# First batch of an attention and expert kernel: W1 fetched in row chunks, its projection split by head group, and the first layer run without other matmuls in between

## The chip, the cores and the metric

The kernel runs on one core of one Trainium2 chip, as one launch. The metric is the device time of that launch in microseconds (us). TensorE does the matmuls (PE in the profile, its weight loads PEld), VectorE is DVE, ScalarE is ACT, GpSimd is POOL, and SyncE (SP) issues most transfers.

## The reference

A linear attention over 32 memory slots feeds a mixture of experts in which every token goes to one expert:

```python
a = softmax(phi, axis=seq)                                # B, H, S, 32
k_m, v_m = einsum(a, k), einsum(a, v)                     # B, H, 32, 64
attn = softmax(q @ k_m.T / sqrt(64))                      # B, H, S, 32
x = (attn @ v_m) transposed to (B * S, H * 64)            # tokens
logits = normalized(x) @ normalized(expert_emb).T / tau
e = argmax(logits); gate = softmax(logits)[e]
out[token] = gate * (relu(x @ w1[e]) @ w2[e])             # w1: 512 x 1024, w2: 1024 x 512
```

There are B = 8 batches of S = 576 tokens, H = 8 heads and 8 experts.

## The kernel before, in words

The program goes through the batches one after the other. For each batch it computes the slot sums, the scores, the attention weights `aw` (softmaxed and transposed by DVE), and picks one expert for the whole batch. Since a token is its attention weights times `v_m`, `x @ w1` is computed as `aw @ (v_m @ w1)`: the **projection** (tiles `pg`, copied by ACT into `gh` and by DVE, as the rounding rest, into `gl`) multiplies the 32 slots of each head by W1, and the **first layer** (tiles `ph`) multiplies the attention weights `aT` by `gh` and `gl`. The second layer (tiles `py`) uses W2 in a rounded part `wh` and a rest `wl`, both made on POOL and ACT (`split_w`).

The eight heads form two groups g of four. In the projection each head is a matmul with 64 rows and 32 columns of the array, and `heads` gives each of the eight heads a place (row half, column quarter) of its own; the four heads of one group take four of these eight places. W1 of the chosen expert is four chunks c of 128 rows by 1024 columns in `w1s`; group 0 reads chunks 0 and 1, group 1 reads chunks 2 and 3. The projection has two column halves k of 512; a tile `pg_kg` is one half of one group.

The first layer makes 16 tiles, `ph_sf` (token half s, eighth f of the 1024 features), six matmuls each; after each one ACT writes `hh` (for s = 1 also `h4`) and DVE writes the rest `hl`. It is a generator: `batch` calls the steps that are listed for number n after tile n, and this hand-written list sets the order of all other work on every engine. The tiles `pg`, `tt` and `ph` share four PSUM banks in turn (`mm`), so a tile waits until the one four turns earlier has been read.

Only batch 0 is touched. There, `pairs` multiplies `aw` by `vv` for five token tiles i and two groups g (tiles `po`, 40 matmuls), from which DVE makes the logits `lg` and the best expert `oh`; `turned` transposes `aw` (tiles `tt`, copied by ACT into `ea`); `norm` forms squared token norms from `po` and `ea` on DVE (two instructions with an accumulator read each for every token tile); `total` counts the votes, and `late` gives the gates in small DVE instructions after tiles 4 to 9. `owner` compares the votes with the count that chose the expert (`key`, in PSUM). In the order before, tile `pg` of column half 0 stands ahead of `pairs`, and half 1 stands between `ph_01` and `ph_02`; `tt` stands after `ph_00` and after `ph_02`.

Of the kernel before, what the change touches and what calls it, by code (L numbers as in the profile page):

```python
# [8 lines left out]
F32 = mybir.dt.float32  # L9
# [4 lines left out]
ALU = mybir.AluOpType  # L14
AX = mybir.AxisListType
# [4 lines left out]
P = 128  # L20
B, H, S, D, M = 8, 8, 576, 64, 32
N, DM, E, FF = B * S, H * D, 8, 1024
NG = 2
NC = 4
T0 = (0, 128, 256, 384, 512)
S2 = S + 64
NT = len(T0)
BL = S // 32
HS = S // 2
# [17 lines left out]
class Tokens:  # L47
# [79 lines left out]
    def pairs(self):  # L127

        k, nc, b, d, ps = self.k, self.nc, self.b, D + E, self.ps
        at = lambda i, h: ps[2 * (i // 3) + h][:, 2 * d * (i % 3) :][:, : 2 * d].rearrange("p (g m) -> p g m", g=NG)  # L130
        for i in range(NT):
            for g in range(NG):
                for h, c in ((0, 0), (1, 0), (0, 1), (1, 1)):
                    r, to = slice(64 * h, 64 * h + 64), slice(64 * c, 64 * c + 64)
                    nc.tensor.matmul(
                        at(i, h)[to, g],
                        lhsT=k.aw[r, g, T0[i] + 64 * c : T0[i] + 64 * c + 64],
                        rhs=k.vv[r, g, D * h : D * h + d],
                        start=True,
                        stop=True,  # L140
                    )
            self.po[i] = [at(i, h)[..., E * h :][..., :D] for h in range(2)]
        self.room = ps[-1][:, 512 - E :]
        l2 = k.wk.tile([P, NT, E], F32, tag="l2", name=f"l2{b}")
        for n, i in enumerate((slice(0, 3), slice(3, NT))):
            for h, to in enumerate((self.lg, l2)):
                e = ps[2 * n + h][:, : 2 * d * (i.stop - i.start)].rearrange("p (i g m) -> p i m g", g=NG, m=d)
                e = e[:, :, D - D * h :][:, :, :E]
                nc.vector.tensor_reduce(out=to[:, i], in_=e, axis=AX.X, op=ALU.add)
        nc.vector.tensor_tensor(out=self.lg, in0=self.lg, in1=l2, op=ALU.add)  # L150
        self.best(*range(NT))
# [62 lines left out]
    def total(self):  # L214
        self.all = self.count(self.room, range(NT))
        self.flags()

    def owner(self):
        k, nc, b = self.k, self.nc, self.b
        cm = k.wk.tile([P, 1], F32, tag="cm", name=f"cm{b}")  # L220
        self.own = k.wk.tile([P, E], F32, tag="own", name=f"own{b}")
        nc.vector.tensor_reduce(out=cm, in_=self.key, axis=AX.X, op=ALU.max)
        nc.vector.tensor_scalar(out=self.own, in0=self.key, scalar1=cm, scalar2=None, op0=ALU.is_equal)

    def flags(self):

# [46 lines left out]
class Kernel:  # L273
# [161 lines left out]
    def load_w1(self, e, halves=False):  # L435

        for k in range(2 if halves else 4):
            c, f = (slice(NC), slice(512 * k, 512 * k + 512)) if halves else (slice(k, k + 1), slice(FF))
            self.nc.sync.dma_start(self.w1s[:, c, f], self.w1[bass.ds(e, 1), :, c, f].rearrange("a p c f -> (a p) c f"))

    def load_w2(self, e, n=2):
        nc = self.nc
# [209 lines left out]
    def project(self, n, vT, room=None):  # L652

        nc = self.nc
        for k in range(2):
# [8 lines left out]
                )  # L664
            yield

    def first(self, n):

        nc = self.nc
        gh, gl, (ah, al) = self.gh, self.gl, self.aT  # L670
        for s in range(2):
            to = slice(s * HS, s * HS + HS)
            for f in range(8):
                p = self.mm([P, HS], f"ph{n}_{s}{f}")
                fs = slice(f * P, f * P + P)
                for g in range(NG):
                    for k, (w, x) in enumerate(((gh, ah), (gh, al), (gl, ah))):
                        nc.tensor.matmul(  # L678
                            p, lhsT=w[:, g, fs], rhs=x[:, g, to], start=g == 0 and k == 0, stop=g == 1 and k == 2
                        )  # L680
                nc.scalar.activation(self.hh[:, f, to], p, AF.Relu)  # L681
                if s:
                    nc.scalar.activation(self.h4[:, f], p[:, HS - 64 :], AF.Relu)
                nc.vector.scalar_tensor_tensor(  # L684
                    out=self.hl[:, f, to], in0=p, scalar=0.0, in1=self.hh[:, f, to].bitcast(F32), op0=ALU.max, op1=ALU.subtract
                )
                yield
# [52 lines left out]
    def steps(self, b, t, u):  # L740


        first, second = ([[] for _ in range(n)] for n in (16, 40))

        for j in range(8):
            at = first[j] if b else first[2] if j < 2 else first[8 + j]
            at.append(lambda j=j: self.split_w(self.nc.gpsimd.tensor_copy if b or j < 6 else None))
        if not b:
            late = t.late()
            first[0].append(lambda: t.turned(1, 2))  # L750
            first[1] += [lambda: list(self.second_part), lambda: t.norm(1, 2)]
            first[2] += [lambda: t.turned(3, 4), t.total]
            first[3] += [lambda: t.norm(3, 4), lambda: self.load_kv(2)]
            for f in range(4, 10):
                first[f].append(lambda: next(late))
            first[12] += [lambda: self.keep(0), lambda: self.load_q(2)]
        if u:
            c, o = b + 1, 0 if b else 3
            if not b:
                first[9].append(lambda: self.scores(c))  # L760
            for k in range(2):
                first[(3 + k if b else 9 + 2 * k)].append(lambda k=k: self.results(c, k))

            places = (first[6], first[8], first[10], first[12]), (first[12], first[14], second[0], second[3])
            if not b:
                places = (second[3], second[3], second[3], second[7]), (second[7], second[7], second[7], second[10])
            all = slice(0, BL)
            for g in range(NG):
                work = u.weigh((g,), all)
                places[g][0].append(lambda g=g: u.fill((g,), all, [self.sT[:, i] for i in range(NG)]))  # L770
                for at in places[g][1:]:
                    at.append(lambda work=work: next(work, None))
            for at, g in zip((second[0], second[3]) if b else (second[7], second[10]), range(NG)):
                at.append(lambda g=g: (u.divide((g,), all), u.lay(g), u.turn((g,), all)))
            o = 0 if b else 7
            m = b + 2
            if m < B:
                for g in range(NG):
                    second[11 + 3 * g + o].append(lambda g=g: self.softmax(m, (g,)))
                second[16 + o].append(lambda: self.shares(m))  # L780
                second[17 + o].append(lambda: self.visit(u, m))
                second[(21 if b else 19) + o].append(lambda: self.gather(u, m))
                second[(28 if b else 25) + o].append(lambda: self.load_phi(m + 1))
                second[(31 if b else 28) + o].append(lambda: self.load_kv(m + 1))
            else:
                second[17].append(u.attend)
                second[20].append(lambda: self.load_w2(u.choose(), 8))
                second[37].append(lambda: list(self.project(c, self.vT[c % 2], self.pt)))
            o = 0 if b else 2
            second[22 + o].append(self.parts)  # L790
            second[22 + o if b else 30].append(lambda: self.keep(c))
            second[23 + o + (not b)] += [u.owner, u.flags]
            for n, i in enumerate(((0, 1), (2, 3), (4,))):
                second[24 + n + o + (not b)].append(lambda i=i: u.norm(*i))
            after = u.late()
            for n in (27, 28, 29, 30, 31, 32):
                second[n + o].append(lambda: next(after))
            second[32 + o].append(lambda: list(after))
        return first, second
# [19 lines left out]
    def batch(self, b, t, u):  # L819
# [8 lines left out]
        if b and u:  # L828
            self.keys(b + 1)
            self.values(b + 1)  # L830
        project = self.project(b, self.vT[b % 2]) if u else ()
        if b:
            list(project)
            if u:
# [1 line left out]
        else:  # L836
            self.keys(1)
            self.values(1, copy=self.nc.scalar.copy)
            next(project)
            self.second_part = project  # L840
            for g in range(NG):
                self.part(g, slice(P, HS), self.nc.scalar.copy)
            t.attend()
            for g in range(NG):
                self.part(g, slice(HS, S), self.nc.scalar.copy)
            t.norm(0)
        for n, _ in enumerate(self.first(b)):
            for step in first[n]:
                step()
# [132 lines left out]
def moe_linformer(ctx, tc, phiT, qT, kv, kvt, emb, tau, w1, w2, out):  # L982
# [67 lines left out]
    for g in range(NG):  # L1050
        next(weights[g])
        list(weights[g])
    t.owner()
    k.shares(1, v=k.nc.gpsimd)
    for g in range(NG):
        k.part(g, slice(0, P), k.nc.scalar.copy)
    k.slots(1, accs)
    k.tags = 4
    k.scale(1)
# [41 lines left out]
```

## Time and profile before

| what | value |
|---|---|
| time, median of 3 runs | 405.27 us (404.66 to 405.93) |
| profiled execution | 406.18 us, of which the span from first to last instruction is 404.4 us |
| PE busy | 393.8 us (97%) |
| DVE, ACT, POOL busy | 261.3, 158.7, 171.5 us |
| TensorE clock granted | 0.996 of full speed |
| the stretch of the change | 28 to 50 us of the span |

A busy share is the time in which an engine has at least one instruction in flight. Matmuls overlap, so the time that one takes from its neighbours is the distance between starts, not its own duration.

### The profile page before, as it was taken

How to read it: one execution, taken by the hardware profiler on the slowest of the kernel's cores; microseconds unless marked ns; L12 is line 12 of the kernel's file. 1: busy time of each engine (PE TensorE's matmuls, PEld its weight loads, DVE VectorE, ACT ScalarE, POOL GpSimd, SP SyncE). 2: the span in 40 equal slices, each digit the busy share in tenths (PEclk: the TensorE clock that was granted, in tenths of full speed). 3: DMA queues.
4: the chain of work that ended last, by engine and by line, in shares of the span. 5: the costliest groups of instructions: out<-in, count | busy, mean ns of one | idle time of the engine just before them, and what ended most of it. 6: DMA issues, size and time to landing. Idle time of an engine off the chain costs nothing. (4 is left out here: it accounts for less than half of the span.)

```text
span 404.4 us, 10470 instructions
## 1 busy us (share of the span) xinstructions
PE 393.8 (97%) x3997; PEld 317.8 (79%) x3997; DVE 261.3 (65%) x917; ACT 158.7 (39%) x432; POOL 171.5 (42%) x205
## 2 busy tenths in 40 slices
PE   7889999999999999999999999999999999999995
PEld 3358878788887978879787988879788897879784
DVE  4688895779665793758745795657937595745000
ACT  4366723165313633147311753137231561146110
POOL 1036482187133940369121960349303781329300
PEclk9999999999999999999999999999999999999998
DMA  8989936997679935996459947799349504790011
GB/s 261 323 325 381 356 108 160 307 363 283 129 242 383 380 56 121 331 389 253 75 176 344 371 182 158 221 391 366 58 125 342 210 2 79 242 405 4 15 52 56
DMA packets 69430, 91.24 MB, mean 226 GB/s; under 512 B 41752, under 2 KB 47640, under 8 KB 69248
## 3 DMA queue, kind: packets, MB, share of 16 engines
q1 hardware_dynamic: 66496, 82.00, 61.8%
q0 software_dynamic: 2688, 8.26, 5.7%
q8 instruction: 32, 0.52, 0.5%
q10 hardware_dynamic: 192, 0.28, 0.3%
q14 instruction: 22, 0.18, 0.1%
HBM read 71.19 MB, written 19.33 MB: 224 GB/s over the span
## 5 line engine op out<-in xcount | busy, mean ns | idle before, releaser
L678 PE MATMUL ph<-aT,gh 128*128 128x288 f32 x512 | 103.2, 297 | 0.0
L731 PE MATMUL py<-wh,hh 128*128 128x512 f32 x248 | 99.3, 400 | 0.0
L731 PE MATMUL py<-wh,hl 128*128 128x512 f32 x248 | 96.7, 390 | 0.0
L731 PE MATMUL py<-wl,hh 128*128 128x512 f32 x248 | 96.7, 390 | 0.0
L649 POOL TENSOR_TENSOR wl<-w2s,wh 128x512 fp32r<-128x512 f32 x64 | 85.4, 1336 | 5.0
L678 PEld LDWEIGHTS ph<-aT,gh 128*128 128x128 f32 x512 | 81.8, 188 | 1.7 <-issue 0.8
L678 PE MATMUL ph<-aT,gl 128*128 128x288 f32 x256 | 75.4, 294 | 0.0
L684 DVE SCALAR_TENSOR_TENSOR hl<-ph,hh 128x288 fp32r<-128x288 f32 x128 | 56.0, 450 | 21.5 <-ACT hh L681 16.5
L681 ACT ACTIVATE hh<-ph 128x288 fp32r<-128x288 f32 x128 | 52.3, 416 | 33.2 <-PE ph L678 32.9
L736 ACT ACTIVATE ys<-py,gate 128x512 f32<-128x512 f32 (+1 forms) x39 | 25.1, 643 | 100.9 <-PE py L731 89.2
L869 POOL DMA_DIRECT2D out_dram<-ys x28 | 15.5, 555 | 101.0 <-ACT ys L736 85.3
L731 PEld LDWEIGHTS py<-wh,hh 128*128 128x128 f32 x248 | 46.5, 188 | 14.6 <-issue 5.1
L731 PEld LDWEIGHTS py<-wh,hl 128*128 128x128 f32 x248 | 46.6, 188 | 10.1
L731 PEld LDWEIGHTS py<-wl,hh 128*128 128x128 f32 x248 | 46.6, 188 | 9.0
L678 PEld LDWEIGHTS ph<-aT,gl 128*128 128x128 f32 x256 | 48.0, 188 | 0.0
L639 POOL TENSOR_TENSOR aT<-aw,aT 128x576 fp32r<-128x576 f32 (+3 forms) x20 | 23.7, 1202 | 49.4 <-DVE aT L638 45.9
L648 POOL CAST wh<-w2s 128x512 fp32r<-128x512 f32 x62 | 38.5, 622 | 2.6 <-DMA w2s<-w 2.5
L720 PE MATMUL py<-w2s,h 128*64 128x256 f32 x256 | 29.4, 382 | 0.0
L662 DVE TENSOR_TENSOR gl<-pg,gh 128x512 fp32r<-128x512 f32 x32 | 19.9, 682 | 8.6 <-ACT gh L661 8.6
L720 PEld LDWEIGHTS py<-w2s,h 128*64 128x64 f32 x256 | 17.7, 137 | 9.3 <-DVE hl L684 1.0
L469 ACT ACTIVATE ex<-ex,nm 128x576 f32<-128x576 f32 x16 | 12.3, 771 | 28.0 <-DVE nm L454 27.9
L661 ACT CAST gh<-pg 128x512 fp32r<-128x512 f32 x32 | 16.5, 599 | 9.4 <-PE pg L659 9.4
(175 smaller groups left out, 467.2 us busy)
## 6 DMA issues: line engine op xcount, KB each, us to landing
kx<-kv SPq DMA_DIRECT2D x32, 512.0 KB, 7.4
w2s<-w SPq DMA_DIRECT2D x28, 512.0 KB, 9.9
w1s<-w SPq DMA_DIRECT2D x28, 512.0 KB, 7.0
out_dram<-ys POOLq DMA_DIRECT2D x28, 256.0 KB, 6.2
qt<-qT SPq DMA_DIRECT2D x12, 576.0 KB, 8.3
ad<-aw SPq DMA_DIRECT2D x8, 576.0 KB, 12.0
td<-x SPq DMA_DIRECT2D x56, 72.0 KB, 2.1
ea<-td SPq DMA_DIRECT2D x7, 512.0 KB, 4.7
```

What stands on the lines that cost most here:

```text
L639: self.nc.gpsimd.tensor_tensor(out=al, in0=a, in1=ah.bitcast(F32), op=ALU.subtract)
L648: (copy or self.nc.scalar.copy)(h, x)
L649: self.nc.gpsimd.tensor_tensor(out=l, in0=x, in1=h.bitcast(F32), op=ALU.subtract)
L661: nc.scalar.copy(self.gh[:, g, f], ps[g])
L662: nc.vector.tensor_tensor(out=self.gl[:, g, f], in0=ps[g], in1=self.gh[:, g, f].bitcast(F32), op=ALU.subtract)
L678: nc.tensor.matmul(p, lhsT=w[:, g, fs], rhs=x[:, g, to], start=g == 0 and k == 0, stop=g == 1 and k == 2)
L681: nc.scalar.activation(self.hh[:, f, to], p, AF.Relu)
L684: nc.vector.scalar_tensor_tensor(out=self.hl[:, f, to], in0=p, scalar=0.0, in1=self.hh[:, f, to].bitcast(F32), op0=ALU.max, op1=ALU.subtract)
L720: nc.tensor.matmul(p[64 * j : 64 * j + 64], lhsT=self.h4[:, f], rhs=self.w2s[:, f, d * j : d * j + d], start=f == 0, stop=f == 7,)
L731: nc.tensor.matmul(p, lhsT=h[:, f, to], rhs=w[:, f], start=f == 0 and k == 0, stop=f == 7 and k == 2)
L736: nc.scalar.activation(y[:, :d], p, AF.Copy, scale=gate[:, i : i + 1])
L869: eng.dma_start(self.out[r : r + P], y)
```

## The change

Four edits, all for batch 0. `load_w1` still makes two transfers of 1 MB, but each has two whole chunks of W1 (8 KB in one run per partition) instead of half of the columns of all four (four runs of 2 KB per partition). `pairs` goes through all token tiles of group 0 first, then all of group 1. A new function `grouped` makes the projection by group: both column halves of group 0 ahead of `pairs`, both of group 1 behind it. The steps that stood between the first tiles of the first layer move: both `turned` calls stand around the second group's projection, `norm` and the copies of the last 288 token columns of `aT` go behind tiles `ph_00` and `ph_01`, and `owner` goes behind `ph_02`; for that ACT copies `key` to SBUF (`held`).

```diff
-        for i in range(NT):
-            for g in range(NG):
+        order = [(i, g) for i in range(NT) for g in range(NG)]
+        for i, g in order if b else sorted(order, key=lambda o: o[1]):
...
+    def kept(self):
+        self.held = self.k.wk.tile([P, E], F32, tag="held", name="held")
+        self.nc.scalar.copy(self.held, self.key)
...
-            c, f = (slice(NC), slice(512 * k, 512 * k + 512)) if halves else (slice(k, k + 1), slice(FF))
-            self.nc.sync.dma_start(self.w1s[:, c, f], self.w1[bass.ds(e, 1), :, c, f].rearrange("a p c f -> (a p) c f"))
+            c = slice(2 * k, 2 * k + 2) if halves else slice(k, k + 1)
+            self.nc.sync.dma_start(self.w1s[:, c], self.w1[bass.ds(e, 1), :, c].rearrange("a p c f -> (a p) c f"))
...
+    def grouped(self, n, vT):
+
+        nc = self.nc
+        halves = slice(0, 512), slice(512, FF)
+        for g in range(NG):
+            ps = [self.mm([P, 512], f"pg{n}_{k}{g}") for k in range(2)]
+            for k, f in enumerate(halves):
+                for h, j, r, c, i in self.heads((g,)):
+                    nc.tensor.matmul(ps[k][j], lhsT=vT[r, g, c % 2, i], rhs=self.w1s[r, c, f], start=True, stop=True)
+            for k, f in enumerate(halves):
+                nc.scalar.copy(self.gh[:, g, f], ps[k])
+                nc.vector.tensor_tensor(
+                    out=self.gl[:, g, f], in0=ps[k], in1=self.gh[:, g, f].bitcast(F32), op=ALU.subtract
+                )
+            yield
...
-            first[0].append(lambda: t.turned(1, 2))
-            first[1] += [lambda: list(self.second_part), lambda: t.norm(1, 2)]
-            first[2] += [lambda: t.turned(3, 4), t.total]
+            first[0].append(lambda: t.norm(0, 1))
+            for g in range(NG):
+                first[1].append(lambda g=g: self.part(g, slice(HS, S), self.nc.scalar.copy))
+            first[1] += [lambda: t.norm(2)]
+            first[2] += [t.owner, t.total]
...
             t.attend()
-            for g in range(NG):
-                self.part(g, slice(HS, S), self.nc.scalar.copy)
-            t.norm(0)
+            t.turned(1, 2)
+            list(project)
+            t.turned(3, 4)
...
-    t.owner()
...
+    t.kept()
```

On TensorE, between the slot sums of batch 1 and the first layer of batch 0, the order before is this:

```order
L659 MATMUL pg_00_502<-w1s,vT_80 32x512 x4
L659 MATMUL pg_01_503<-w1s,vT_80 32x512 x4
...
L678 MATMUL ph_00_578<-aT_85,gl 128x288
L168 MATMUL tt_1_587<-ident,aw 128x128 x4
L678 MATMUL ph_01_593<-aT_85,gh 128x288
...
L659 MATMUL pg_10_602<-w1s,vT_80 32x512 x4
L659 MATMUL pg_11_603<-w1s,vT_80 32x512 x4
L678 MATMUL ph_02_620<-aT_85,gh 128x288
...
L168 MATMUL tt_3_633<-ident,aw 128x128 x4
```

The same place in the changed kernel; the 40 matmuls of `pairs` stand where the first line of dots is:

```order
L680 MATMUL pg_00_500<-w1s,vT_80 32x512 x4
L680 MATMUL pg_10_501<-w1s,vT_80 32x512 x4
...
L168 MATMUL tt_1_570<-ident,aw 128x128 x4
L680 MATMUL pg_01_576<-w1s,vT_80 32x512 x4
L680 MATMUL pg_11_577<-w1s,vT_80 32x512 x4
L168 MATMUL tt_3_590<-ident,aw 128x128 x4
L699 MATMUL ph_00_596<-aT_85,gh 128x288
...
L699 MATMUL ph_01_609<-aT_85,gh 128x288
```

Each `x4` is four heads; a pair of rows was two groups at one half, and is now one group at two halves. The two transposes `tt` and the second pair have left the first layer.

On DVE, behind the choice of the best expert (`oh`), the order before is this:

```order
L158 TENSOR_TENSOR oh_211<-lg_207,m_210 128x40
L177 ISA ea,s_209<-po_0_520,ea 128x2x64
...
L684 SCALAR_TENSOR_TENSOR hl<-ph_00_578,hh 128x288
L684 SCALAR_TENSOR_TENSOR hl<-ph_01_593,hh 128x288
L662 TENSOR_TENSOR gl<-pg_10_602,gh 128x512
L662 TENSOR_TENSOR gl<-pg_11_603,gh 128x512
...
L684 SCALAR_TENSOR_TENSOR hl<-ph_02_620,hh 128x288
L227 SCALAR_TENSOR_TENSOR fl<-po_3_523,own_408 128x8
L684 SCALAR_TENSOR_TENSOR hl<-ph_03_646,hh 128x288
```

In the changed kernel it is this, with the norms of tiles 0 and 1 at the first line of dots and of tile 2 at the second:

```order
L683 TENSOR_TENSOR gl<-pg_01_576,gh 128x512
L683 TENSOR_TENSOR gl<-pg_11_577,gh 128x512
L705 SCALAR_TENSOR_TENSOR hl<-ph_00_596,hh 128x288
...
L705 SCALAR_TENSOR_TENSOR hl<-ph_01_609,hh 128x288
...
L705 SCALAR_TENSOR_TENSOR hl<-ph_02_624,hh 128x288
L227 TENSOR_REDUCE cm_637<-held 128x1
L228 TENSOR_SCALAR own_638<-held,cm_637 128x8
L232 SCALAR_TENSOR_TENSOR fl<-po_3_521,own_638 128x8
L705 SCALAR_TENSOR_TENSOR hl<-ph_03_648,hh 128x288
```

The norm of tile 0 stood ahead of the first `hl` and now stands behind it, and the two instructions of `owner` have come in between `ph_02` and `ph_03`. On POOL the order is the same as before.

## Rows read from the trace of the kernel before

**Rows 1.** Waits of PE from 28 us to the end: total, times, longest
```profile
PE po L135 <- DVE aw L92: 0.3, 1, 0.3
PE po L501 <- ACT ex L469: 0.2, 1, 0.2
```

**Rows 2.** PE in order of time: start, length, instruction, count, idle time before
```profile
29.00 1.09 PE L659 MATMUL pg<-w1s,vT 64*32 64x512 f32 x16
30.02 0.61 PE L135 MATMUL po<-vv,aw 64*64 64x72 f32 x24
30.91 1.43 PE L135 MATMUL po<-vv,aw 64*64 64x72 f32 x56 [0.28 <-DVE aw L92]
32.27 0.54 PE L678 MATMUL ph<-aT,gh 128*128 128x288 f32 x2
...
33.17 0.60 PE L168 MATMUL tt<-ident,aw 128*128 128x128 f32 x4
33.53 0.51 PE L678 MATMUL ph<-aT,gh 128*128 128x288 f32 x2
...
34.49 1.51 PE L659 MATMUL pg<-w1s,vT 64*32 64x512 f32 x16
35.93 0.54 PE L678 MATMUL ph<-aT,gh 128*128 128x288 f32 x2
...
36.83 0.60 PE L168 MATMUL tt<-ident,aw 128*128 128x128 f32 x4
...
37.42 0.51 PE L678 MATMUL ph<-aT,gh 128*128 128x288 f32 x2
...
38.30 0.43 PE L678 MATMUL ph<-aT,gh 128*128 128x288 f32 x2
...
39.09 0.42 PE L678 MATMUL ph<-aT,gh 128*128 128x288 f32 x2
```

**Rows 3.** PE and its weight loads, narrow windows: passes of array-place matmuls
```profile
29.45 0.64 PE L659 MATMUL pg<-w1s,vT 64*32 64x512 f32 x8
...
34.49 0.63 PE L659 MATMUL pg<-w1s,vT 64*32 64x512 f32 x4
...
34.49 1.08 PE L659 MATMUL pg<-w1s,vT 64*32 64x512 f32 x12
...
34.94 0.15 PEld L659 LDWEIGHTS pg<-w1s,vT 64*32 64x32 f32 x8 [0.29 <-DVE hl L684]
```

**Rows 4.** W1 in batch 0: SP's first issue, and the transfers' time to landing
```profile
23.30 0.62 SPq L439 DMA_DIRECT2D w1s<-w  x1
...
w1s<-w SPq DMA_DIRECT2D x2, 1024.0 KB, 5.2
```

**Rows 5.** Page's L681 (mean ns); all L150 (ns min/median/max); DVE and PE in time
```profile
L681 ACT ACTIVATE hh<-ph 128x288 fp32r<-128x288 f32 x128 | 52.3, 416 | 33.2 <-PE ph L678 32.9
...
L150 DVE TENSOR_TENSOR lg<-lg,l x8: 199/201/639, 32.7 to 343.8; 128x40 f32<-128x40 f32 x8
...
37.47 0.28 DVE L177 CUSTOM_DVE_ANT_1 ea<-po,ea 128x128 f32<-128x128 f32 x1
...
38.31 0.45 DVE L684 SCALAR_TENSOR_TENSOR hl<-ph,hh 128x288 fp32r<-128x288 f32 x1
...
38.95 0.46 DVE L684 SCALAR_TENSOR_TENSOR hl<-ph,hh 128x288 fp32r<-128x288 f32 x1
...
46.82 0.46 DVE L684 SCALAR_TENSOR_TENSOR hl<-ph,hh 128x288 fp32r<-128x288 f32 x1 [0.16 <-ACT h L683]
...
47.71 0.43 PE L678 MATMUL ph<-aT,gh 128*128 128x288 f32 x2
```

**Rows 6.** POOL in order of time; last row the page's group of L649
```profile
31.50 2.53 POOL L639 TENSOR_TENSOR aT<-aw,aT 128x160 fp32r<-128x160 f32 x4 [2.93 <-ACT aT L638]
...
45.85 0.20 POOL L260 TENSOR_SCALAR idx<-m 128x5 f32<-128x5 f32 x1 [6.06 <-DVE m L259]
...
L649 POOL TENSOR_TENSOR wl<-w2s,wh 128x512 fp32r<-128x512 f32 x64 | 85.4, 1336 | 5.0
```

More of the change, by code (lines that the diff above doesn't have):

```diff
@@ L130, in pairs @@
         at = lambda i, h: ps[2 * (i // 3) + h][:, 2 * d * (i % 3) :][:, : 2 * d].rearrange("p (g m) -> p g m", g=NG)
-        for i in range(NT):
-            for g in range(NG):
[L133 to L141, printed above, removed]
+        order = [(i, g) for i in range(NT) for g in range(NG)]
+        for i, g in order if b else sorted(order, key=lambda o: o[1]):
+            for h, c in ((0, 0), (1, 0), (0, 1), (1, 1)):
+                r, to = slice(64 * h, 64 * h + 64), slice(64 * c, 64 * c + 64)
+                nc.tensor.matmul(
+                    at(i, h)[to, g],
+                    lhsT=k.aw[r, g, T0[i] + 64 * c : T0[i] + 64 * c + 64],
+                    rhs=k.vv[r, g, D * h : D * h + d],
+                    start=True,
+                    stop=True,
+                )
             self.po[i] = [at(i, h)[..., E * h :][..., :D] for h in range(2)]
@@ L221, in owner @@
         self.own = k.wk.tile([P, E], F32, tag="own", name=f"own{b}")
-        nc.vector.tensor_reduce(out=cm, in_=self.key, axis=AX.X, op=ALU.max)
-        nc.vector.tensor_scalar(out=self.own, in0=self.key, scalar1=cm, scalar2=None, op0=ALU.is_equal)
+        key = self.key if b else self.held
+        nc.vector.tensor_reduce(out=cm, in_=key, axis=AX.X, op=ALU.max)
+        nc.vector.tensor_scalar(out=self.own, in0=key, scalar1=cm, scalar2=None, op0=ALU.is_equal)
     def flags(self):
@@ L665, in project @@
             yield
+    def grouped(self, n, vT):
[10 more added lines that the diff above has]
+                    out=self.gl[:, g, f], in0=ps[k], in1=self.gh[:, g, f].bitcast(F32), op=ALU.subtract
+                )
+            yield
     def first(self, n):
@@ L830, in batch @@
             self.values(b + 1)
-        project = self.project(b, self.vT[b % 2]) if u else ()
+        project = (self.project if b else self.grouped)(b, self.vT[b % 2]) if u else ()
         if b:
@@ L839, in batch @@
             next(project)
-            self.second_part = project
             for g in range(NG):
```

## The prediction

> **What bounds the kernel now.** I read the list of PE's waits first. From 28 us to the end of the span PE waited for a named engine twice, 0.5 us in all [rows 1]: once for the transposed weights `aw` in the stretch of the change, once for ACT's exponentials of a later batch. Behind the change there is next to nothing that could swallow a delay or hold back a gain, so what the stretch from 29 to 50 us wins or loses on PE reaches the end almost whole. Then I read PE in order of time [rows 2]: the first `pg` pair starts at 29.00, `pairs` runs from 30.02 to 32.27 with the 0.28 us wait in it, and `ph_00`, `tt`, `ph_01`, the second `pg` pair, `ph_02` and `tt` follow without a gap; `ph_03` starts at 37.42. The question is how many microseconds of PE lie between 29.00 and `ph_03` after the change. Last I read DVE and POOL there, since their order moves too.
>
> **The change part by part.**
>
> *The projection by group.* This is the largest term, and it is a loss. The places on the array decide it: a pair of tiles used to be two groups, eight heads in eight places; now it is one group at two column halves, and both halves need the same four places one after the other. The trace shows how long a turn takes. The matmuls are fp32 and come in two records each, one per pass. In the first pair eight heads start at 29.00 and their second pass (eight records) at 29.45 [rows 2, 3]: 0.45 us a pass. In the second pair the four heads of one tile started alone at 34.49, because the other tile's bank still waited for DVE's `hl`; by 35.2 twelve had started, the next weights having been let in at 34.94, and the last four came after that [rows 3]. So four heads alone hold the array for the same 0.45 us as eight: the second pair needed three passes, 34.49 to 35.93, 1.44 us, where the first needed two, 29.00 to 30.02, 1.02 us [rows 2]. After the change each pair has two halves times two passes in the same places, four passes. First pair 2 to 4: +0.90 us. Second pair 3 to 4: +0.45 us. Together **+1.35 us**. From below this cost is nil, if the halves could share a place after all; the staggered second pair speaks against it. From above it is 1.5 us, if the second pair costs as much more as the first did with its start and end.
>
> *`pairs` by group.* Of 80 records 56 took 30.91 to 32.27, 1.36 us, or 24.3 ns each [rows 2]; 80 without a wait are 1.94 us against 2.25 now. With the first pair ending at 30.92, both groups of `aw`, which let PE go on at 30.91 before, are there. **-0.31 us.** Most of this would come from the longer first pair alone, whatever the order.
>
> *The breaks.* An uninterrupted tile of the first layer takes 0.79 us, 38.30 to 39.09. `ph_00` took 0.90 (to 33.17), `ph_01` 0.96 (33.53 to 34.49), `ph_02` 0.90 (35.93 to 36.83), each entered from other matmuls [rows 2]. Afterwards only `ph_00` is entered from something else; `ph_01` takes 0.79 and `ph_02`, which the vote count still follows, 0.79 to 0.90. 2.76 us become about 2.54: **-0.22 us**. The two `tt` stay at about 0.36 us each (33.17 to 33.53) wherever they stand. [...]
>
> *Sum on PE:* 1.35 - 0.31 - 0.22 = **+0.8 us** at `ph_03`, which would start near 38.2.
>
> *What must be ready for `ph_00`.* It now needs `gh` and `gl` of both groups. ACT and DVE make the second group's first half while PE runs the second half (0.90 us) and `tt` (0.36 us), and `ph_00` reads `gl` of group 1 only in its sixth matmul; I cost this at nothing. If that cover were short, the wait would be some tenths, once.
>
> *W1 in whole chunks.* Same bytes, same two issues. The first was issued at 23.30 and landed 5.2 us later, at 28.5 [rows 4], and PE waited for no transfer [rows 1], so a faster one gains nothing and a slower one has 0.5 us of room. The second is needed only near 33.2 now. **0.** Transfers behind them may land a little earlier; nobody on PE waits for them.
>
> *`held`, `owner`.* ACT's small copy lies in front of its wait for the slot sums; `owner` leaves a place on DVE where the next instruction waits for POOL anyway, and comes back behind `ph_02`, where DVE is busy. It is counted there.
>
> *DVE behind `ph_00`.* By the sums above `ph_00` starts at 29.00 + 1.92 + 1.94 + 0.36 + 1.89 + 0.36 = 35.47. Its `hl` can start after 0.90 us of matmuls, some 0.2 to drain and ACT's 0.42 [rows 5], near 37.0. Then up to the `hl` of `ph_03` DVE has three norms at 0.42 (two took 37.47 to 38.31), one `hl` with `fl` at 0.64 (38.31 to 38.95), two more `hl` at about 0.42 and `owner` at about 0.4 (an estimate: two small instructions): 3.1 us. So that `hl` starts near 40.1 instead of 38.95 [rows 5]: DVE is 1.2 us late where PE is 0.8 late. It then works without rest to the `hl` of `ph_12`, which ends at 47.28 and whose bank `ph_16` takes at 47.71 [rows 5]. The room is 0.43 us, and 0.16 of idle time ahead of that `hl`; the extra 0.4 us just fits. But POOL moves too: its last `aT` rests now wait for ACT behind `ph_01`, near 38.5 instead of 32, so the first W2 pieces run until about 44, into the 6.06 us in which POOL stood idle before [rows 6]. During that DVE does the small steps of `late`, some with two SBUF inputs. One such instruction, L150, took 639 ns in batch 0, while POOL worked, and 201 in the other batches [rows 5, 6]: 0.44 us lost. A single POOL rest lasts 1.34 us [rows 6], so one blocked instruction costs DVE 0 to 1.3 us; what exceeds the room lands on PE. Bounds for PE: 0 and 0.7; I take **+0.2 us**, nearer to the row in which one blocked instruction cost 0.44 us.
>
> **Sum:** +0.8 + 0.2 = +1.0 us. The profiled execution has 406.18 us, 404.4 of span and 1.8 around it, and lies 0.9 above the median of the runs; it would become 407.2. On the median, 405.27 becomes **406.3 us**, 0.25% more. A measurement of this kernel can tell about 0.3%, 1.2 us, from no change.
>
> **The rivals.**
>
> 1. *The forecast*, PE +0.8 and little more, 405.9 to 406.5: chance 0.52.
> 2. *Slower: DVE becomes the bound in the first layer.* Place: the `hl` of `ph_12`, ahead of `ph_16` (or that of `ph_05`, ahead of `ph_11`). Price: one or two blocked steps of `late`, together 0.6 to 1.4 us less the room of about 0.2 that is left, so +0.4 to +1.2 on top of 0.8: 406.5 to 407.3. It decides as soon as DVE loses more than 0.4 us to POOL. For it: L150, and POOL's shift into its idle time. Against it: most steps have one input or read PSUM, and the blocked ones may fall between POOL's instructions. [...] Chance 0.33.
> 3. *Faster: the four extra passes cost nothing*, the two halves of a group overlapping like the two groups did. Then there are four passes in place of five: -0.45 - 0.31 - 0.22, 404.3 us, -0.25%, which still counts as no change unless earlier data bring another 0.2 us. For it: nothing but that the places are not seen in the trace. Against it: the staggered pair. Chance 0.08.
> 4. *Nothing comes through:* half of the extra passes fits into time that PE loses today without a record, about 405.3. Against it: PE's waits. Chance 0.07.
>
> **How the numbers follow.** The likeliest case gives 406.3. Its own range is 405.7 to 406.7 with the scatter of a median. To hold 8 in 10 the range must take in most of rival 2 and rival 4: 405.0 to 407.3. Faster by more than 0.3% (under 404.05) needs rival 3 and luck: 0.05. Slower by more than 0.3% (over 406.49) is most of rival 2 and the upper edge of the forecast: 0.38. The rest, 0.57, is no change.
>
> **What the profile after would show.** The first pair: 16 records whose starts fall at four times 0.45 us apart, the next matmul near 30.9. `pairs` without a wait, about 1.94 us. The second pair about 1.9 us. `ph_01` at 0.79 us behind `ph_00`. `ph_03` near 38.2; the tile after it and the end of the span later by the same amount. For rival 2: a wait of PE on `hl` or a gap before `ph_11` or `ph_16`, and a small DVE instruction of `late` over 400 ns. The prediction is wrong if the first pair ends at 30.0 to 30.1 (rival 3), if `ph_00` waits for `gl`, or if the pair waits for W1.

## The result and the profile after

The changed kernel took 408.19 us (median of 8 runs, 407.11 to 408.97) where the kernel before took 405.13 us beside it (8 runs, 404.08 to 406.00): a ratio of 1.0058, 95% interval 1.0036 to 1.0080. It is slower, by more than the forecast of +1.0 us and beyond its range of 405.0 to 407.3 us. A second set of runs gave 1.0035 (1.0016 to 1.0053). The profiled execution took 408.91 us with a span of 407.0 us, at a granted clock of 0.999.

Waits of PE from 28 us to the end in the changed kernel (total, times, longest), the answer to [rows 1]:

```profile
PE ph L699 <- DVE hl L705: 0.9, 1, 0.9
PE acc L524 <- issue: 0.3, 1, 0.3
PE po L506 <- ACT ex L474: 0.2, 1, 0.2
```

The wait for `aw` is gone and a larger one has come, of a first-layer tile for DVE's `hl`. Its place is seen on PE in order of time, beside [rows 2]:

```profile
28.89 1.92 PE L680 MATMUL pg<-w1s,vT 64*32 64x512 f32 x16
30.74 1.48 PE L135 MATMUL po<-vv,aw 64*64 64x72 f32 x80
32.15 0.66 PE L168 MATMUL tt<-ident,aw 128*128 128x128 f32 x4
32.73 1.92 PE L680 MATMUL pg<-w1s,vT 64*32 64x512 f32 x16
34.59 0.66 PE L168 MATMUL tt<-ident,aw 128*128 128x128 f32 x4
35.00 0.51 PE L699 MATMUL ph<-aT,gh 128*128 128x288 f32 x2
...
35.88 0.42 PE L699 MATMUL ph<-aT,gh 128*128 128x288 f32 x2
...
36.66 0.43 PE L699 MATMUL ph<-aT,gh 128*128 128x288 f32 x2
...
37.63 0.51 PE L699 MATMUL ph<-aT,gh 128*128 128x288 f32 x2
...
41.66 0.43 PE L699 MATMUL ph<-aT,gh 128*128 128x288 f32 x2
...
43.57 0.54 PE L699 MATMUL ph<-aT,gh 128*128 128x288 f32 x2 [0.94 <-DVE hl L705]
...
66.66 0.66 PE L506 MATMUL te<-ident,ex 64*128 64x64 f32 x16
```

The row at 37.63 is `ph_03`: 8.74 us after the first `pg`, where [rows 2] give 37.42 - 29.00 = 8.42. So far the change has cost only 0.32 us. The tile at 41.66 is `ph_10`, the next one `ph_11`; a tile takes 0.79 us undisturbed, this step takes 1.91, so 1.1 us are lost at `ph_11`. The last row is the first transpose for the slot sums of batch 1 (`te`), behind both layers of batch 0: 37.77 us after the first `pg`. In the kernel before it stands 35.92 us after it:

```profile
64.92 0.66 PE L501 MATMUL te<-ident,ex 64*128 64x64 f32 x16
```

The stretch has lost 1.85 us, which both intervals hold.

What DVE did before that `hl`, in the changed kernel:

```profile
41.06 0.16 DVE L239 TENSOR_TENSOR ss<-s 128x5 f32<-128x5 f32 x1
41.26 0.53 DVE L240 TENSOR_SCALAR ss<-ss 128x5 f32<-128x5 f32 x1
41.82 0.17 DVE L38 TENSOR_SCALAR nrg<-ss 128x5 int32<-128x5 int32 x1
42.03 1.13 DVE L39 TENSOR_SCALAR nrg<-nrg 128x5 int32<-128x5 int32 x1
43.07 0.44 DVE L705 SCALAR_TENSOR_TENSOR hl<-ph,hh 128x288 fp32r<-128x288 f32 x1
```

and in the kernel before, where L235 is the same instruction as L240 now:

```profile
40.72 0.17 DVE L235 TENSOR_SCALAR ss<-ss 128x5 f32<-128x5 f32 x1
...
41.13 0.17 DVE L39 TENSOR_SCALAR nrg<-nrg 128x5 int32<-128x5 int32 x1
```

Two instructions on five elements per partition grew from 0.17 to 0.53 and 1.13 us, 1.32 us together. POOL in the changed kernel, the answer to [rows 6]:

```profile
37.67 1.59 POOL L644 TENSOR_TENSOR aT<-aw,aT 128x288 fp32r<-128x288 f32 x2 [4.88 <-ACT aT L643]
39.19 0.63 POOL L653 CAST wh<-w2s 128x512 fp32r<-128x512 f32 x1
39.90 1.30 POOL L654 TENSOR_TENSOR wl<-w2s,wh 128x512 fp32r<-128x512 f32 x1
41.15 0.61 POOL L653 CAST wh<-w2s 128x512 fp32r<-128x512 f32 x1
41.84 1.29 POOL L654 TENSOR_TENSOR wl<-w2s,wh 128x512 fp32r<-128x512 f32 x1
47.71 0.20 POOL L265 TENSOR_SCALAR idx<-m 128x5 f32<-128x5 f32 x1 [4.58 <-DVE m L264]
```

L240 starts while the cast of 41.15 runs and ends at 41.79, as the cast does (41.76). L39 starts while the rest of 41.84 runs and ends at 43.16, the rest at 43.13. Between them L38 took its usual 0.17. Before, POOL was idle during all of these, for the 6.06 us up to 45.85, so from 39.79 on [rows 6]. Both times the DVE instruction ends 0.03 us after the POOL instruction that was running when it started, as if it had waited for that end, though it has only five elements per partition. POOL isn't seen to wait in turn: L38 starts 0.02 us ahead of the rest of 41.84, which still takes its usual 1.29 us.

Two more profiles of the changed kernel, below, show the same wait. Another 1.2 us or so that this execution loses after batch 0 doesn't recur in them: from the first `pg` to the end of the span it has 407.0 - 28.89 = 378.1 us, the other two 376.8 and 376.9; two profiles of the kernel before have 375.4 and 376.2. Against the first profile of before it loses 0.5 us between the `te` of batches 1 and 2 and 0.6 us between those of 4 and 5. The second profile of the kernel before loses 0.4 and 0.3 us at the same places, so such losses come without the change too. The eight runs of the changed kernel fall in two groups, 407.1 to 407.7 and 408.7 to 409.0; the profiled execution is of the upper one.

### The profile page after: what moved, and what is told of

Its sections match the earlier page's. It is cut to its first block, busy times and chain, and to the rows that moved or that the text cites. A ratio compares the mean times of both kernels' runs of the same rounds, so it can differ in the third digit from the quotient of the medians.

```text
span 407.0 us, 10470 instructions
## 1 busy us (share of the span) xinstructions
PE 394.6 (97%) x3997; PEld 318.7 (78%) x3997; DVE 262.3 (64%) x917; ACT 158.4 (39%) x433; POOL 171.8 (42%) x205
## 5 line engine op out<-in xcount | busy, mean ns | idle before, releaser
L654 POOL TENSOR_TENSOR wl<-w2s,wh 128x512 fp32r<-128x512 f32 x64 | 84.2, 1317 | 5.0
L653 POOL CAST wh<-w2s 128x512 fp32r<-128x512 f32 x62 | 40.1, 647 | 1.2 <-DMA w2s<-w 1.1
L667 DVE TENSOR_TENSOR gl<-pg,gh 128x512 fp32r<-128x512 f32 x28 | 17.4, 683 | 7.8 <-ACT gh L666 7.8
L177 DVE CUSTOM_DVE_ANT_1 ea<-po,ea 128x128 f32<-128x128 f32 x80 | 17.6, 285 | 0.0
```

The lines of the kernel that those rows point to most:

```text
L177: nc.vector.tensor_tensor_reduce(out=to, in0=y, in1=to, scale=1.0, scalar=0.0, op0=ALU.mult, op1=ALU.add, accum_out=self.s2[:, h, i : i + 1],)
L653: (copy or self.nc.scalar.copy)(h, x)
L654: self.nc.gpsimd.tensor_tensor(out=l, in0=x, in1=h.bitcast(F32), op=ALU.subtract)
L667: nc.vector.tensor_tensor(out=self.gl[:, g, f], in0=ps[g], in1=self.gh[:, g, f].bitcast(F32), op=ALU.subtract)
```

## The experiments

All changes are made in batch 0 alone. The table gives places in time from the profile of each kernel, in us after its first `pg`, which itself falls anywhere from 27.0 to 29.15 us in the runs; "steps" are L240 and L39 (L235 and L39 in versions of before), in ns. The fourth column is the difference of the two before it.

| kernel | `ph_03` | `te` | between | steps | ratio to before (95%) |
|---|---|---|---|---|---|
| before | 8.42 | 35.92 | 27.50 | 171, 172 | |
| before, another profile | 8.51 | 36.25 | 27.74 | 173, 173 | |
| changed | 8.74 | 37.77 | 29.03 | 526, 1130 | 1.0058 (1.0036 to 1.0080) |
| changed, second set | 8.74 | 37.76 | 29.02 | 500, 1132 | 1.0035 (1.0016 to 1.0053) |
| changed, third profile | 8.74 | 37.76 | 29.02 | 521, 1132 | |
| changed, `aT` early again | 9.16 | 36.92 | 27.76 | 172, 172 | 1.0009 (0.9992 to 1.0027) |
| changed, column halves again | 8.94 | 37.98 | 29.04 | 525, 1128 | 1.0022 (1.0003 to 1.0041) |
| changed, weight split late | 8.73 | 39.98 | 31.25 | 171, 173 | |
| before, `aT` late | 7.79 | 36.87 | 29.08 | 524, 1134 | 1.0011 (0.9995 to 1.0028) |
| before, `pairs` by group | 8.89 | 36.63 | 27.74 | 172, 172 | |
| before, W1 in chunks | 11.79 | 39.42 | 27.63 | 171, 170 | |
| before, both halves first | 8.43 | 35.93 | 27.50 | 171, 173 | 1.0015 (0.9991 to 1.0038) |
| before, half 1 behind `pairs` | 8.25 | 35.74 | 27.49 | 170, 172 | 0.9988 (0.9968 to 1.0008) |
| the same, by groups and chunks | 8.73 | 36.22 | 27.49 | 172, 173 | 1.0001 (0.9980 to 1.0022) |

**The changed kernel a second time.** No edit.

> The changed kernel once more, for a second profile beside those of this call. Both theories: 0.4% to 0.8% slower than before. The DVE theory (POOL's W2 pieces, which now fall into the steps of `late`, hold up one-input DVE instructions that read and write SBUF) expects again a wait of PE near 1 us ahead of `ph_11` and the two small instructions L240 and L39 well over their 0.17 us. What lies behind batch 0 (0.5 us for W1 of batch 1, 0.6 us in the slot sums of batch 4) need not come back.

407.42 us against 406.28, 0.35% by the ratio, a little less than expected, and the wait of 0.9 us stands in the same place. The loss is real.

**The changed kernel with the copies of `aT` early again.** One part undone, so that POOL's work comes early as before:

```diff
-            for g in range(NG):
-                first[1].append(lambda g=g: self.part(g, slice(HS, S), self.nc.scalar.copy))
...
             t.attend()
+            for g in range(NG):
+                self.part(g, slice(HS, S), self.nc.scalar.copy)
```

> The changed kernel, but ACT's copies of the last 288 token columns of aT stand behind `pairs` again, so POOL does their rests and the first two W2 pieces early. DVE theory: L240 and L39 back to 0.17 us, no wait ahead of `ph_11`, 1.1 to 1.5 us faster than the changed kernel, that is 0.2% to 0.3% over before. Pass theory (the time goes into the extra passes of the projection alone): as slow as the changed kernel, ratio 1.006.

Both steps are back at 172 ns, PE doesn't wait for `hl`, and `te` comes 0.85 us sooner: 1.26 us won between `ph_03` and `te`, less 0.42 lost ahead of `ph_03`. That 0.42 is a pause in `pairs`, for which the profile names no engine:

```profile
30.79 0.97 PE L135 MATMUL po<-vv,aw 64*64 64x72 f32 x47
31.97 0.73 PE L135 MATMUL po<-vv,aw 64*64 64x72 f32 x33 [0.21 <-issue]
```

**The changed kernel with the projection by column halves.** The places of the heads and W1's transfers as before, all else changed:

```diff
-            c = slice(2 * k, 2 * k + 2) if halves else slice(k, k + 1)
+            c, f = (slice(NC), slice(512 * k, 512 * k + 512)) if halves else (slice(k, k + 1), slice(FF))
...
-        project = (self.project if b else self.grouped)(b, self.vT[b % 2]) if u else ()
+        project = self.project(b, self.vT[b % 2]) if u else ()
```

> The changed kernel, but the projection goes by column halves over both groups again, in eight places, and W1 comes by column halves; all else stays moved. Pass theory: four passes instead of eight, `ph_03` 1.6 to 1.8 us earlier than in the changed kernel, and the time with it, 0.4% under the changed kernel. DVE theory: `ph_03` as early as that, but the wait ahead of `ph_11` stays near 1 us or grows, because POOL still comes late; 0.1% to 0.4% under the changed kernel.

Each pair takes two passes, 1.02 us, and yet nothing is won by `te`; the 1.6 us that I expected at `ph_03` did not come. The wait for `hl` is unchanged. Ahead of `ph_03` `pairs` takes 2.13 us instead of 1.41, with pauses, and PE now comes too early for W1:

```profile
31.97 1.09 PE L664 MATMUL pg<-w1s,vT 64*32 64x512 f32 x16 [0.77 <-DMA w1s<-w]
```

So the four extra passes aren't what makes DVE late.

**The kernel before with the copies of `aT` late.** The one part alone:

```diff
+            for g in range(NG):
+                first[1].append(lambda g=g: self.part(g, slice(HS, S), self.nc.scalar.copy))
...
             t.attend()
-            for g in range(NG):
-                self.part(g, slice(HS, S), self.nc.scalar.copy)
```

> The kernel before with one edit alone: ACT's copies of the last 288 token columns of aT stand behind `ph_01` and the second projection instead of behind `pairs`, so POOL's two rests and the first two W2 pieces fall into the steps of `late`. DVE theory: L235, L38 or L39 grow from 0.17 to 0.4 to 1.3 us, PE waits 0.5 to 1.2 us on `hl` before `ph_11` or `ph_12`, and the transposes of the next slot sums start 0.5 to 1.2 us later after the first projection matmul than the 35.9 us of before; 0.1% to 0.3% slower. Rival (DVE is late only because the norms went behind `ph_00`): no wait of PE, no change.

This edit by itself brings the loss. DVE there, then POOL, then PE:

```profile
40.25 0.34 DVE L234 TENSOR_TENSOR ss<-s 128x5 f32<-128x5 f32 x1
40.62 0.52 DVE L235 TENSOR_SCALAR ss<-ss 128x5 f32<-128x5 f32 x1
...
41.38 1.13 DVE L39 TENSOR_SCALAR nrg<-nrg 128x5 int32<-128x5 int32 x1
```

```profile
39.26 1.30 POOL L649 TENSOR_TENSOR wl<-w2s,wh 128x512 fp32r<-128x512 f32 x1
40.51 0.61 POOL L648 CAST wh<-w2s 128x512 fp32r<-128x512 f32 x1
41.20 1.29 POOL L649 TENSOR_TENSOR wl<-w2s,wh 128x512 fp32r<-128x512 f32 x1
```

```profile
42.93 0.53 PE L678 MATMUL ph<-aT,gh 128*128 128x288 f32 x2 [0.76 <-DVE hl L684]
```

From `ph_03` to `te` it takes 29.08 us where the kernel before took 27.50, the same 1.5 us that the changed kernel lost there (29.03). L234, with two SBUF inputs, takes longer here too (0.34 us for 0.16) and ends at 40.59, the rest on POOL at 40.56. In time the edit costs less than it does by `te`, and the interval reaches past 1; the trace carries the verdict here.

**The changed kernel with POOL idle during `late`.** The first two pieces of the weight split go from step 2 to step 10:

```diff
-            at = first[j] if b else first[2] if j < 2 else first[8 + j]
+            at = first[j] if b else first[10] if j < 2 else first[8 + j]
```

> The changed kernel with the first two pieces of the next weight split moved from step 2 to step 10 of the row, so POOL has only `aT` and the index ahead of the statistics. Theory (POOL's piece is what holds up L240 and L39): both take about 0.17 us, and `ph_11` doesn't wait for `hl`; the matmuls of the second layer may then wait for the weights split late, by about 2 us. Rival (the order of DVE itself makes `hl` late): L240 and L39 may be short, but `ph_11` still waits 0.9 us.

The order on DVE and the late `aT` stay; only POOL's pieces are gone from the window. The steps take 171 and 173 ns, and `ph_11` doesn't wait. POOL does the pieces behind the index instead, and PE waits for them in the second layer (the row on `pg` below is the first pair, early in this run for W1):

```profile
45.46 0.20 POOL L265 TENSOR_SCALAR idx<-m 128x5 f32<-128x5 f32 x1 [7.14 <-DVE m L264]
45.73 0.61 POOL L653 CAST wh<-w2s 128x512 fp32r<-128x512 f32 x1
```

```profile
PE py L752 <- POOL wl L654: 2.4, 4, 1.2
PE pg L680 <- DMA w1s<-w: 0.5, 1, 0.5
```

The pieces are the cause, then, and they can't simply be put off: the new wait of 2.4 us is dearer than the old.

**The kernel before with `pairs` by group, and with W1 in chunks.** Each part alone, with the edits as in the diff of the change. The projection stays in column halves, so with W1 in chunks its first pair needs both transfers.

> The kernel before with `pairs` by group alone. The attention weights of group 0 are ready first, so the wait of 0.28 us shrinks or moves; 40 matmuls take between 1.4 us (as in the changed kernel) and 2.2 us (as before). If the order by group made them fast, `pairs` ends 0.3 to 0.8 us earlier after the first projection matmul than the 3.3 us of before; if the longer first pair made them fast, it ends where it did.

> The kernel before with W1 in whole chunks alone: each column half then needs both transfers. The second transfer's data ended near 31 to 32 us in all profiles so far, so the first pair waits for W1 1.5 to 3 us, and the time grows by 1 to 2.5 us. If the form of the transfer mattered by itself, the second transfer would land clearly earlier than 31 us.

By group, `pairs` still waits 0.23 us for `aw` and then has a pause of 0.99 us with no engine named, again after 47 records; the order of the loop saved nothing. W1 in chunks alone makes PE wait for the second transfer in the first pair:

```profile
31.01 1.93 PE L659 MATMUL pg<-w1s,vT 64*32 64x512 f32 x8 [1.94 <-DMA w1s<-w]
```

The chunk form needs the grouped projection; that transfer is there at 31.0, before the changed kernel asks for it at 32.73.

**The kernel before with both halves ahead of `pairs`, and with half 1 behind it.** Both keep the eight places, the column halves and the early `aT`, and run the first layer without breaks. The first calls `list(project)` ahead of `attend`; of the second the core is:

```diff
-            first[0].append(lambda: t.turned(1, 2))
-            first[1] += [lambda: list(self.second_part), lambda: t.norm(1, 2)]
-            first[2] += [lambda: t.turned(3, 4), t.total]
+            first[0].append(lambda: t.norm(1))
+            first[1].append(lambda: t.norm(2))
+            first[2] += [t.total]
...
+            t.turned(1, 2)
+            list(project)
+            t.turned(3, 4)
```

> The kernel before, with both column halves of the projection in eight places ahead of `pairs`, both `turned` behind it, the first layer without breaks, but the aT copies kept early and the norms of tiles 0 to 2 near their old place; W1 by column halves. Both theories: PE loses the 0.28 us wait in `pairs`, the third pass of the second pair (0.45 us) and the breaks (0.2 us): 0.9 us faster than before, 0.2%. DVE theory adds: no blocked step of `late`, since POOL ends its first W2 pieces by 40 us. Pass theory alone would allow a wait on `hl`.

> The kernel before, projection by column halves in eight places, the second half behind `pairs` and the first two transposes, the first layer without breaks, aT copies early, norms of tiles 1 and 2 behind `ph_00` and `ph_01`. From the first projection matmul `ph_03` starts 7.5 to 8.0 us later (8.4 before, 8.7 in the changed kernel), with no wait on `hl`; the transposes of the next slot sums 0.4 to 0.9 us earlier than before, and the time 0.1% to 0.2% under before. If DVE alone is late because of the norms, there is a wait before `ph_11` and nothing is won.

With both halves first PE waits 2.7 us for W1, and nothing is won. With half 1 behind `pairs` it waits for no transfer, and no `hl` is late. `te` is 0.18 us earlier than before, less than I expected and less than two profiles of the kernel before differ from each other (0.33), and the interval of the ratio includes 1. Freed of its expensive parts the idea of the change is worth nothing that can be measured.

**The same by groups and chunks.** That version with W1 in chunks and `grouped`, so that only the extra passes differ:

> The version with the second half behind `pairs` and no breaks, with one thing changed: W1 arrives in whole chunks and the projection goes by group of heads. Theory (the rest of the change's loss is its four extra passes; the DVE wait at `ph_11` comes only from the `aT` copies put late): no wait of `ph` on `hl`, the one-input DVE instructions at 0.17 us, and the slot sums' transposes of batch 1 about 36.7 to 37.1 us after the first `pg` (35.74 without the grouping, 37.8 in the changed kernel), so 406.3 to 406.8 us at a before of 406.0. Rival (the grouped order itself leads to the DVE wait): the wait is there without the late `aT`, and the transposes come at 37.6 or later.

No wait for `hl`, the steps at 172 ns, so the grouped order alone doesn't lead to the loss. The passes cost 0.48 us by `te`, less than I expected, for the reason seen in `pairs`. In the grouped version, and then in the one without groups:

```profile
28.55 1.92 PE L675 MATMUL pg<-w1s,vT 64*32 64x512 f32 x16
30.40 1.48 PE L135 MATMUL po<-vv,aw 64*64 64x72 f32 x80
31.81 0.66 PE L168 MATMUL tt<-ident,aw 128*128 128x128 f32 x4
```

```profile
27.71 1.09 PE L659 MATMUL pg<-w1s,vT 64*32 64x512 f32 x16
28.73 0.94 PE L135 MATMUL po<-vv,aw 64*64 64x72 f32 x24
29.97 1.11 PE L135 MATMUL po<-vv,aw 64*64 64x72 f32 x56 [0.30 <-DVE aw L92]
31.00 0.66 PE L168 MATMUL tt<-ident,aw 128*128 128x128 f32 x4
```

The longer first pair costs 0.83 us (1.85 against 1.02), and `pairs` behind it gives 0.86 us back (1.41 against 2.27). In these two profiles the first pair's extra passes were free; only the second pair's show (1.86 us, 32.39 to 34.25, for 1.02, 31.59 to 32.61), less 0.3 that the tiles up to `ph_03` took less. It is no rule: with the long first pair `pairs` took 1.41 us in five profiles, but 1.85 with `aT` early again; with the short one it took 2.13 to 3.13 us in five, but 1.46 in the kernel before with `aT` late (left out are the two versions in which PE waited over 1 us for W1 there).

**The kernel before, and the changed kernel, once more.** No edits.

> The kernel before, unchanged, for the scatter of its places in time: both theories expect `ph_03` 8.4 us, the end of the first half of the second layer 20.4 us and the next transposes 35.9 us after the first `pg`, each within 0.1 us, while the start of the first `pg` may move by about 1 us.

> The changed kernel, unchanged, a third time: the wait of `ph` on `hl` again 0.9 us, the transposes 37.8 us after the first `pg`, within 0.1 us; the span follows from when the first `pg` starts.

The changed kernel repeats to 0.01 us. The kernel before does not repeat to the 0.1 us that I expected: `te` is 0.33 us later than in its first profile. Here PE started the first `pg` 2.0 us sooner, and `pairs` stopped twice:

```profile
28.02 0.67 PE L135 MATMUL po<-vv,aw 64*64 64x72 f32 x24
28.99 0.60 PE L135 MATMUL po<-vv,aw 64*64 64x72 f32 x23 [0.30 <-DVE aw L92]
29.99 0.85 PE L135 MATMUL po<-vv,aw 64*64 64x72 f32 x33 [0.40 <-issue]
...
32.99 1.09 PE L659 MATMUL pg<-w1s,vT 64*32 64x512 f32 x16
34.01 0.53 PE L678 MATMUL ph<-aT,gh 128*128 128x288 f32 x2
```

The second pair takes 1.02 us here, two passes, not the 1.44 us of [rows 2].

Against this profile the stretch of the changed kernel lost 1.5 us, against the other 1.85. Differences under about 0.3 us in the table mean nothing.

## Why the prediction was wrong

**The step that failed** is the term "DVE behind `ph_00`". It saw POOL's pieces move into `late`, and it gave the price of a blocked instruction as 0 to 1.3 us, but it let only instructions with two SBUF inputs be blocked, of which L150 was the one row; it took one at 0.44 us, less the room, and put +0.2 us on PE, with 0.7 as the upper bound. The runs show two one-input instructions held up, L240 and L39, by 0.36 and 0.96 us, and 1.1 us lost on PE, more than the bound. The exclusion, "most steps have one input or read PSUM", was argued from no row. The run bears out its second half for `hl`, which reads `ph` in PSUM: the four that started between 37.73 and 40.70 us, while POOL worked from 37.67 to 41.20, took 0.45 us each, as one did in the kernel before with POOL idle (0.45 at 41.21). Its first half is what failed. In batch 0 of the kernel before POOL stood idle whenever those steps ran, so that stretch could not have shown them blocked. The same step in later batches could. Its shortest, median and longest time over the eight batches (ns), and one of the long ones:

```profile
L235 DVE TENSOR_SCALAR ss<-ss x8: 171/290/302, 40.7 to 349.8; 128x5 f32<-128x5 f32 x8
```

```profile
118.92 0.56 POOL L869 DMA_DIRECT2D out_dram<-ys  x1
...
119.17 0.29 DVE L235 TENSOR_SCALAR ss<-ss 128x5 f32<-128x5 f32 x1
```

In five batches this one-input step took 290 to 302 ns, each time while POOL was issuing a transfer (L869), in the other three 171 to 173, in one of them beside such an issue too. That POOL was the reason there is not shown, but the row spoke against the exclusion, and these steps should have been in the bound. With 1.32 us in it, less the room of about 0.2, the term would have come to about 1.1. That is rival 2, and its bracketed place: the `hl` of `ph_05`, ahead of `ph_11`. I gave it 0.33; from its own condition, "as soon as DVE loses more than 0.4 us to POOL", it deserved most of the chance. The main place that I named, `ph_16`, lost only 0.17 us.

**The rest of that term.** DVE was less late than I had it. Two of its small terms are as the traces have them: in the kernel before the tile behind `ph_03` starts at 38.30 and ACT's `hh` of `ph_03` at 38.50, the 0.2 us that I set between matmuls and ACT, and the two steps of `owner` took 0.15 and 0.23 us in the changed kernel, for about 0.4. The `hl` of `ph_03` came 39.49 - 28.89 = 10.60 us after the first `pg`, before 9.95 [rows 5]: 0.65 us, not 1.2. POOL's rests of `aT` started at 37.67 (I said near 38.5) and the first two W2 pieces ended at 43.13 (near 44). What the term lacked beside the two instructions is 0.4 us after `ph_11`, in small pauses up to `te` (the 0.17 at `ph_16` among them), which no row puts down to an engine. Versions with an early `aT` take 27.49 to 27.76 us from `ph_03` to `te`, those with a late one and POOL's pieces behind it 29.02 to 29.08.

**The projection by group** was right: 1.85 us (28.89 to 30.74) and 1.86 us (32.73 to 34.59) are four passes each. Over [rows 2] that is +0.83 and +0.42, 1.25 us for 1.35 forecast. The three passes of the second pair before, though, were those of one execution: over the second profile of the kernel before, with 1.02 us, it is +0.84.

**`pairs`** was mis-sized: 1.41 us (30.74 to 32.15), not 1.94, so -0.84 us for -0.31 (over the second profile of before, with 2.75 us, it is -1.34). Without a pause a record takes 17.6 ns (1.41 us / 80). The 56 records from which I took 24.3 ns would then have needed 0.99 us of their 1.36; the rest is pauses that the row doesn't show. The break before the last 33 records in the second profile of before is such a pause, long enough to be printed.

**The breaks** gave -0.09 us, not -0.22: from the end of `pairs` to `ph_03`, without the second pair, PE took 3.62 us (0.58 to 32.73 and 3.04 from 34.59), before 3.71 (5.15 from 32.27, less 1.44) [rows 2]. `ph_01` did get shorter, by 0.18 us (35.88 to 36.66), but the first `tt` took 0.58 us behind `pairs` (32.15 to 32.73) where it took 0.36 behind `ph_00` [rows 2]. So the price moved to the first `tt` instead of going away, 0.22 us for 0.18. The second `tt`, behind `pg`, took only 0.41 us (34.59 to 35.00); what sets such a price no run shows.

**Sum.** 1.25 - 0.84 - 0.09 = +0.32 us on PE up to `ph_03` where +0.8 was forecast, and +1.53 behind it, 1.1 of that at `ph_11`, where +0.2 was: 1.85 instead of 1.0. The PE terms' error hid about a third of the other's. W1 in chunks cost nothing in the changed kernel, as forecast; `ph_00` waited for no `gl`.

What lies beyond the stretch stays open: the first comparison gives +1.5 to +3.2 us, the second +0.7 to +2.2, so 1.85 fits both. But 1.85 on the 405.27 us of the forecast would have given 407.1, inside the range; the first set's median of 408.19 lies higher, its profile loses 1.2 us behind batch 0 that the other two of the changed kernel don't lose, and why is open.

## What to carry to other kernels

Before work is moved to a later time on POOL, list the small DVE instructions that it will then lie beside, one-input `tensor_scalar` on SBUF among them, and price each at what is left of POOL's instruction, not at its own 0.17 us (here two took 0.53 and 1.13); a stretch in which POOL is idle says nothing against it, and the longest time of the same line over all batches may already tell. A rate taken from a long grouped row should be held against the shortest pitch of the same instruction in the trace, since pauses too short to be printed make it look slower (here 24.3 ns a record for 17.6). In five of six profiles here a longer stretch of matmuls ahead won them back (`pairs` at 1.41 us).

## What was not expected of the hardware

A DVE instruction on 5 elements per partition took 1.13 us when it met a POOL instruction with 1.1 us to go, and it did so in each of the five profiles with POOL's pieces there (500 to 526 and 1128 to 1134 ns), in none of the nine without (170 to 173 ns), all in batch 0. `pairs` paused after 47 of its 80 records in five profiles, with either order of the loop; in four of them the pause was long enough to be printed, 0.17 to 0.99 us with no releaser shown. In the nine others it didn't pause there. The traces hold a candidate: in every profile a block of 16 KB arrives on an instruction queue (q8) within 2.1 us of the first `pg`. In the five with the pause record 48 starts 1.21 to 1.48 us after that block has landed, in the nine without it starts 1.46 to 5.26 us after. That fits a wait for instructions, and a longer first pair that gives it time; no run moved the block, so the cause is not shown.
